# Weighing the units of a bank together, and giving transposed weights the room of the raw weights, in an attention and two-MLP kernel

## The chip, the core and the metric

One core of a Trainium2 chip runs the whole program. Its engines are TensorE (PE, with the weight loads listed apart as PEld), VectorE (DVE), ScalarE (ACT), GpSimd (POOL) and SyncE (SP), which here issues every DMA. The metric is the device time of one execution in microseconds.

## The reference

Block-causal attention feeds two MLPs that run one after the other on its output.

```python
B, H, S, D = 4, 8, 576, 64
scores = where(pos_i // 64 >= pos_j // 64, q @ k.T / sqrt(D), -1e9)
attn = exp(scores - max); attn = attn / (sum(attn) + 1e-09)
x = (attn @ v) as (B * S, H * D)         # 2304 x 512, float32
h = x @ moe_w_in                         # 512 x 2048
x = maximum(0.01 * h, h) @ moe_w_out     # 2048 x 512
h = x @ moe2_w_in
out = (h * (1 / (1 + exp(-h)))) @ moe2_w_out
```

## The kernel before

The 2304 tokens are cut into six blocks of 384. The first MLP goes block by block, and each block takes 16 steps: a step has a `first_layer` (4 chunks into the bank `h`), a gate on ACT, a split of the gated values into a rounded part `ghi` and a rest `glo`, and a `second_layer` into four banks (`acc`, `u`). Block 0 multiplies in plain float32; in the blocks 1 to 5 every product is three float32r matmuls of 384 columns (hi by lo, lo by hi, hi by hi), so that a step is 24 of them. The weights come as 64-bit words in 512 KB pieces (`convert`: raw tile `wraw`, then `cy`, `cc` on ACT and DVE). The second MLP works on products of split operands (`product`), and starts when the first ends.

While the first MLP works on block b, attention makes block b+1. It is cut into 120 **units** of up to 128 rows of scores (24 in each of the blocks 1 to 5). A unit runs through this chain: `scores` on PE into a bank `s` (two banks, one or two pieces of the keys), `row_max` on DVE, `expo` on ACT, `norm` on DVE, `p_hi` on ACT or DVE and `p_lo` on DVE (float16 parts `hl`), `turn` (a DMA transpose from `hl` to `pt`, issued by SP), and `values` on PE: three float16 matmuls for each 128 keys into the one bank `x`. Up to three units share a group (the columns of one bank `x`); when its values are in, `take` moves the bank to SBUF (`x_top`, `x_sum`), and the next group may write it. Rooms are rings in SBUF: `hl` and `pt` each hold 2304 float16 columns, and a unit of 576 keys needs 1280 in both, so they hold one such unit, or two to three of fewer keys.

Nothing is ordered by the engines themselves. A planner (`Schedule`) knows a cost for each task, a hop from engine to engine, a rank, and what each task waits for; it writes out the order of each engine once, and each engine then goes through its list in that order. A task that comes late holds all that stands behind it on its engine. SP's list holds all loads, stores and transposes. After the last unit, `end_of_attention` closes attention's rooms; the second MLP's weights (`first_pair`) are loaded into `wraw` by rank, three buffers deep.

Of the kernel before, what the change touches and what calls it, by code (L numbers as in the profile page):

```python
# [19 lines left out]
P = 128  # L20
BLK = 64
# [14 lines left out]
TURN = 0  # L36
COLD = 1.2
# [5 lines left out]
YRINGS = ("ryry", "crcr", "crcr", "crcr", "llcy", "wwww")  # L43
# [14 lines left out]
class Task:  # L58
    def __init__(self, engines, deps, rank, emit):
        self.engines, self.deps, self.rank, self.emit = engines, deps, rank, emit  # L60
        self.users, self.next, self.waits, self.ready, self.end = [], [], 0, 0.0, None
        self.lag = 0


class Schedule:
# [23 lines left out]
    def run(self):  # L89
# [140 lines left out]
def attn_mlp_mlp(  # L230
# [33 lines left out]
    raw = ctx.enter_context(tc.tile_pool(name="raw", bufs=RAWS))  # L264
# [25 lines left out]
    WIDE = {"h0": NC * NB, "h1": NC * NB, "l0": NC * NB, "l1": NC * NB, "cc": CCS * DM}  # L290
    areas, turn_cc = {}, [CCS - 1]
# [5 lines left out]
    def area(name, use, dtype=F32):  # L297

        if (name, use) not in areas:
            n = WIDE.get(name) or SLOTS.get(name, (0, 1))[1] * 2 * DM  # L300
            areas[name, use] = wp.tile([P, n], dtype, tag=name, name=name)
        return areas[name, use]
# [85 lines left out]

    raws, cys, ccs = Turns(RAWS), Turns(CYS), Turns(CCS)

    def convert(src, f, sl, rk, load_rank, to=None, slow=0, lag=0):
# [8 lines left out]
        def load():  # L400
            r = raw.tile([P, DM], I64, tag="wraw", name="wraw")
# [31 lines left out]
        t_load = dma(raw_free, load_rank, DM * P * 8, load, after=raw_after, slow=slow, lag=lag)  # L433
# [251 lines left out]
    hl_ring = ring("hl", HLR, F16)  # L685
    pt_ring = ring("pt", PTR, F16)
    st_ring = ring("st", 64, F32)
    nc.gpsimd.memset(hl_ring.tile, 0.0)
# [7 lines left out]
    class Group:  # L696


        def __init__(self):
            self.x, self.evac = None, []  # L700
# [6 lines left out]
    def attention(blk):  # L707
# [165 lines left out]
        for i in range(0, len(todo), 2):  # L873
# [18 lines left out]
            for bank in banks:  # L892
# [23 lines left out]
                for j, at, a, b, us in taken:  # L916
                    take(pair[j], both, group, at, a, b, us)
            take_pair(pair[0], both)

    def unit(parts, per, rk, group, group_before):  # L920
# [8 lines left out]
        before = units[-1] if units else None  # L929
        r_p, r_hl, r_pt = p_ring.take(n), hl_ring.take(2 * nj * P), pt_ring.take(2 * nj * rows)  # L930
        r_st = st_ring.take(8)
# [5 lines left out]
        pt = pt_ring.view(r_pt, 2 * nj * rows).rearrange("p (a b) -> p a b", b=rows)  # L937
# [3 lines left out]
        def scores(e):  # L941
            u.s = []
            for k0, k1 in cut:
                s = next_s()
                u.s.append(s)
                if native:
                    hd, c0, _ = parts[0]
                    c = c0 - hd.q0
                    k_, q_ = hd.k, hd.q
                    if len(parts) > 1:  # L950
                        k_, q_ = hd.both[:, :n], hd.both[:, n:]
                    nc.tensor.matmul(s[:, :w], q_[:, c : c + P], k_[:, k0:k1], start=True, stop=True)
                    continue
                for i, (hd, c0, _) in enumerate(parts):
                    c = c0 - hd.q0
                    for j, a in enumerate((c, hd.np + c)):
                        nc.tensor.matmul(  # L957
                            s[:, :w], hd.q[:, a : a + P], hd.k[:, k0:k1],
                            start=i + j == 0, stop=i == len(parts) - 1 and j == 1,
                        )  # L960

        def row_max(e):
            if per > BLK:
# [3 lines left out]
            else:  # L967
                for i in range(n_pieces):
                    nc.vector.reduce_max(m2[:rows, i : i + 1], u.s[i][:rows, :w], axis=AX.X)
                nc.vector.tensor_reduce(nm[:rows], m2[:rows], axis=AX.X, op=ALU.max, negate=True)  # L970

        def expo(e):
            for i, (k0, k1) in enumerate(cut):
                nc.scalar.activation(  # L974
                    p[:rows, k0:k1], u.s[i][:rows, :w], AF.Exp, bias=nm[:rows], accum_out=s2[:rows, i : i + 1]
                )
# [23 lines left out]
        def turn():  # L1000
            nc.sync.dma_start_transpose(out=pt, in_=flat[:rows])

        def values(e):
# [3 lines left out]
            for i, (hd, _, c) in enumerate(parts):  # L1007
                for j in range(nj):
# [4 lines left out]
                    hi, lo = pt[:, j, q], pt[:, nj + j, q]  # L1013
# [3 lines left out]
                    nc.tensor.matmul(g.x[:, o], a, lo, start=False, stop=j == nj - 1)  # L1017

        split = [t for hd, _, _ in parts for t in hd.split]
        deps = [*split, before.t_s if before else None]  # L1020
        deps += [o.t_exp for o in (s_users[-2:-1] if n_pieces == 1 else s_users[-2:])]
        s_users.extend([u] * n_pieces)
        m = len(parts)
        time = n_pieces * mm32(w) + 100 if native else 2 * m * n_pieces * mm(w)
        u.t_s = plan.add({"PE": time}, deps, SHORT + rk, scores)
        u.t_max = plan.add({"DVE": 165 + dve_psum(n) + 110 * (n_pieces - 1) * 2}, [u.t_s, *freed(r_st)], rk, row_max)
        deps = [u.t_max, *freed(r_p)]
        u.t_exp = plan.add({"ACT": n_pieces * act(w, True, 2)}, deps, rk, expo)
# [804 lines left out]
```

## Time and profile before

| | us |
|---|---|
| three timed runs, median (lowest, highest) | 973.56 (973.06, 973.63) |
| the profiled execution, its own time | 973.34 |
| its span, first to last instruction | 971.6 |
| PE busy, PEld busy | 945.3, 868.6 |
| DVE busy, ACT busy | 805.1, 563.7 |
| mean granted TensorE clock | 0.994 of full speed |

The profiled execution is 1.7 us longer than its span, and 0.2 us shorter than the median. A matmul's end is modelled, so rows of PE overlap, and busy time hides short stops; the distance from start to start tells more. "Idle before" is the time in which an engine stood still ahead of an instruction, with what released it. Block 1's attention runs from about 40 to 131 us, that of the blocks 2 to 5 from 137 to 517 us, and the second MLP from about 600 us to the end.

### The profile page before, as it was taken

To read this page: it belongs to the slowest core of one execution; us is meant where nothing else is said; L and a number is where in the kernel's file an instruction comes from. 1 tells how busy PE (TensorE), PEld (TensorE's weight loads), DVE (VectorE), ACT (ScalarE), POOL (GpSimd) and SP (SyncE) were. 2 spreads that over 40 slices of the span, in tenths; PEclk is the share of its full clock that TensorE was granted. 3 is DMA by queue.
4 is the path that set the end of the run, shared out by engine and by line. 5 is a ranking of instruction groups with operands and counts; after the bars stand their busy time and mean duration, and the time that the engine had idled before them with its cause. 6 is when DMAs were issued, how large, how long until landed. Compare 5 with 4: busy or idle time off the path is not lost.

```text
span 971.6 us, 18459 instructions
## 1 busy us (share of the span) xinstructions
PE 945.3 (97%) x6531; PEld 868.6 (89%) x6531; DVE 805.1 (83%) x1905; ACT 563.7 (58%) x1258; POOL 36.3 (4%) x127
## 2 busy tenths in 40 slices
PE   7899999999999999999899999999999999999997
PEld 4656567999899999998799999999999999999997
DVE  6888899888888878778682698889899999888865
ACT  6897866766777666667553666655555553221322
POOL 1000000000000001000000000000000000000000
PEclk9899999999999999999999999999999999999999
DMA  7579926676655565566930532678866553443422
GB/s 258 198 183 191 236 67 132 127 132 136 157 134 128 129 157 129 114 143 157 168 86 9 185 115 84 219 250 292 278 216 210 178 166 119 139 151 100 145 65 87
DMA packets 194588, 149.85 MB, mean 154 GB/s; under 512 B 134592, under 2 KB 172480, under 8 KB 194496
## 3 DMA queue, kind: packets, MB, share of 16 engines
q1 hardware_dynamic: 194496, 148.68, 56.6%
q8 instruction: 51, 0.84, 0.4%
q14 instruction: 41, 0.34, 0.1%
HBM read 91.49 MB, written 32.51 MB: 128 GB/s over the span
## 4 chain that ended last, share of the span: by engine, by line
PE 63%; DVE 5%; DMA 2%; issue 1%; ACT 1%; SPq 0%; DVEq 0%; ACTq 0%
PE acc L1257 9%; PE acc L1648 7%; PE s L1648 5%; PE h L1237 4%; PE h L1238 4%; PE h L1239 4%; PE u L1257 3%; PE acc L1485 3%; PE acc L1486 2%; PE acc L1487 2%; PE x L1648 2%; PE u L1648 2%; PE s L957 2%; PE s L1485 2%; PE s L1486 2%; PE s L1487 2%
## 5 line engine op out<-in xcount | busy, mean ns | idle before, releaser
L974 ACT ACTIVATE p<-s,st 128x288 f32<-128x288 f32 (+5 forms) x144 | 73.3, 511 | 40.4 <-DVE st L966 26.5
L988 ACT ACTIVATE hl<-p,st 128x576 f16<-128x576 f32 (+7 forms) x115 | 67.6, 592 | 34.1 <-DVE st L984 10.3
L993 DVE SCALAR_TENSOR_TENSOR hl<-p,st,hl 128x576 f16<-128x576 f32 (+6 forms) x120 | 71.4, 597 | 13.5 <-ACT hl L988 11.6
L1285 ACT ACTIVATE g<-h 128x384 f32<-128x384 f32 x96 | 46.6, 486 | 54.2 <-PE h L1239 47.2
L1015 PE MATMUL x<-pt,v 128*128 128x128 f16 (+1 forms) x432 | 69.4, 212 | 8.8 <-DMA pt<-hl 5.5
L1016 PE MATMUL x<-pt,v 128*128 128x128 f16 (+1 forms) x432 | 67.3, 210 | 0.0
L1257 PE MATMUL acc<-ghi,w 128*128 128x384 f32 x255 | 67.3, 340 | 0.0
L1017 PE MATMUL x<-pt,v 128*128 128x128 f16 (+1 forms) x432 | 66.1, 210 | 0.0
L957 PE MATMUL s<-k,q 128*128 128x288 f32 (+5 forms) x288 | 64.5, 330 | 0.5 <-ACT p L974 0.3
L374 DVE TENSOR_TENSOR glo<-g,ghi 128x384 fp32r<-128x384 f32 x80 | 44.2, 552 | 24.4 <-ACT ghi L363 23.5
L1237 PE MATMUL h<-h,w 128*128 128x384 f32 x180 | 60.9, 338 | 0.0
L1015 PEld LDWEIGHTS <-v 128*128 128x128 bf16 x432 | 41.3, 98 | 21.1 <-issue 10.8
L1537 ACT ACTIVATE e<-e 128x384 f32<-128x384 f32 (+1 forms) x72 | 42.7, 626 | 26.1 <-DVE e L1510 20.7
L1239 PE MATMUL h<-h,w 128*128 128x384 f32 x160 | 53.6, 335 | 0.0
L1238 PE MATMUL h<-l,w 128*128 128x384 f32 x160 | 53.6, 335 | 0.0
L374 DVE TENSOR_TENSOR v<-v 128x320 f32<-128x320 f32 (+5 forms) x112 | 44.3, 423 | 10.0 <-DMA v<-vL 9.3
L409 ACT ACTIVATE cy<-wraw 128x512 f32<-128x512 f32 x64 | 42.7, 669 | 12.2 <-DMA wraw<-w 6.4
L966 DVE TENSOR_REDUCE st<-s 128x1 f32<-128x320 f32 (+5 forms) x96 | 46.5, 485 | 3.1
L1016 PEld LDWEIGHTS <-v 128*128 128x128 bf16 x432 | 41.7, 99 | 7.9 <-issue 7.4
L957 PEld LDWEIGHTS s<-k,q 128*128 128x128 f32 x288 | 43.6, 189 | 2.7 <-ACT p L974 1.7
L1257 PEld LDWEIGHTS acc<-ghi,w 128*128 128x128 f32 x255 | 45.2, 188 | 0.3
L1017 PEld LDWEIGHTS <-v 128*128 128x128 bf16 x432 | 41.4, 98 | 0.0
(368 smaller groups left out, 3016.7 us busy)
## 6 DMA issues: line engine op xcount, KB each, us to landing
wraw<-w SPq DMA_DIRECT2D x64, 512.0 KB, 5.0
a<-g SPq DMA_DIRECT2D x64, 256.0 KB, 3.2
g<-e SPq DMA_DIRECT2D x48, 192.0 KB, 2.9
g<-e SPq DMA_DIRECT2D x24, 384.0 KB, 3.4
kqr<-kq_l SPq DMA_DIRECT2D x16, 480.0 KB, 3.6
kqr<-kq_l SPq DMA_DIRECT2D x16, 416.0 KB, 3.4
v<-vL SPq DMA_DIRECT2D x32, 160.0 KB, 3.1
y<-yT SPq DMA_DIRECT2D x12, 384.0 KB, 3.9
```

Of the source, the lines that this page charges most:

```text
L374: engine[e].tensor_tensor(lo, x, hi, op=ALU.subtract)
L957: nc.tensor.matmul(s[:, :w], hd.q[:, a : a + P], hd.k[:, k0:k1], start=i + j == 0, stop=i == len(parts) - 1 and j == 1,)
L974: nc.scalar.activation(p[:rows, k0:k1], u.s[i][:rows, :w], AF.Exp, bias=nm[:rows], accum_out=s2[:rows, i : i + 1])
L993: nc.vector.scalar_tensor_tensor(hl[:rows, 1, :n], p[:rows], rc[:rows], hl[:rows, 0, :n], op0=ALU.mult, op1=ALU.subtract)
L1015: nc.tensor.matmul(g.x[:, o], a, hi, start=j == 0, stop=False)
L1016: nc.tensor.matmul(g.x[:, o], hd.vb[:, j], hi, start=False, stop=False)
L1017: nc.tensor.matmul(g.x[:, o], a, lo, start=False, stop=j == nj - 1)
L1237: nc.tensor.matmul(h, w1_lo[s.f][:, sl], hi[:, c, : s.n], start=c == 0, stop=False)
L1238: nc.tensor.matmul(h, w1_hi[s.f][:, sl], lo[:, c, : s.n], start=False, stop=False)
L1239: nc.tensor.matmul(h, w1_hi[s.f][:, sl], hi[:, c, : s.n], start=False, stop=c == NC - 1)
L1257: nc.tensor.matmul(s.acc[c][:, : s.n], a, b, start=s.f == 0 and i == 0, stop=s.f == NF - 1 and i == 2)
L1648: nc.tensor.matmul(o, a[:, x], b, start=i == 0 and j == 0 and q == 0, stop=i == NP - 1 and q == 2, skip_group_check=True,)
```

## The change

- `values` of all units of a group becomes one task on PE (`weigh_all`), which waits for all the group's transposes and adds 85 ns (`TRANSIT`) to its planned cost. Of the 128-key slices the first comes first and the others in falling order.
- The raw weights' three buffers become one area `raw`, which serves one after another: raw first-layer weights (and stores of block 0), the transposed weights `pt` of the blocks 2 to 5 (6144 float16 columns), and the second MLP's raw weights. `turn` of the blocks 2 to 5 waits for the last raw users (`raw_done`), and loads into `raw` for the second MLP wait for `end_of_attention` (`raw_later`).
- `hl` and `pt` of block 1 lie in one tile; from block 2 on `hl` has all of it (4608 columns), and its first users wait for block 1's units (`first_units`).
- The planner takes scores and values as ready 700 ns later than its costs say (`SLACK`).
- Scores, maxima and exponentials become one task for each piece; first and second layers become two tasks of two chunks each (`CUTS`).
- `YRINGS`: the blocks 1 to 3 store through `cc` and `cy` only, block 0 through three raw buffers and one `cy`.

```diff
+TRANSIT = 85
+CUTS = ((0, 1), (2, 3))
+SLACK = 700
-YRINGS = ("ryry", "crcr", "crcr", "crcr", "llcy", "wwww")
+YRINGS = ("rrry", "cycy", "cycy", "cycy", "llcy", "wwww")
...
-                heapq.heappush(waiting, (t.ready + (self.HOLD if n else 0), order[id(t)], n, e, t))
+                heapq.heappush(waiting, (t.ready + t.slack + (self.HOLD if n else 0), order[id(t)], n, e, t))
...
+    def raw_room():
+        k = turn_raw[0] = (turn_raw[0] + 1) % RAWS
+        return area("raw", turn_raw[1])[:, k * 2 * DM : (k + 1) * 2 * DM]
...
-        t_load = dma(raw_free, load_rank, DM * P * 8, load, after=raw_after, slow=slow, lag=lag)
+        t_load = dma(raw_free, load_rank, DM * P * 8, load, after=[*raw_after, *raw_later], slow=slow, lag=lag)
...
-    hl_ring = ring("hl", HLR, F16)
-    pt_ring = ring("pt", PTR, F16)
+    halves_tile = pp.tile([P, HLR + PTR], F16, tag="hl", name="hl")
+    hl_first, hl_later = Ring(halves_tile[:, :HLR], HLR), Ring(halves_tile, HLR + PTR)
+    pt_first, pt_later = Ring(halves_tile[:, HLR:], PTR), Ring(None, 4 * DM * RAWS)
...
-                for j in range(nj):
+                order = [0, *reversed(range(1, nj))]
+                for j in order:
...
-        u.t_turn = dma([*padded_keys, *freed(r_pt)], SHORT + rk, 80640 * nj, turn, 1200)
-        evac = group_before.evac if group_before else [x0_free]
-        deps = [u.t_turn, *[t for hd, _, _ in parts for t in hd.v_ready], *evac]
-        u.t_pv = plan.add({"PE": 3 * nj * m * mm16(per)}, deps, SHORT + rk, values)
+        u.t_turn = dma([*padded_keys, *freed(r_pt)], SHORT + rk, 80640 * nj, turn, 1200, () if early else raw_done)
...
+    def weigh_all(group, before):
+        us = group.units
+        deps = [t for u in us for t in (u.t_turn, *[t for hd in u.heads for t in hd.v_ready])]
+        deps += before.evac if before else [x0_free]
+        def values(e):
+            for u in us:
+                u.values(e)
+        t = plan.add({"PE": sum(u.pv_time for u in us) + TRANSIT}, deps, SHORT + us[-1].rk, values)
+        t.slack = SLACK
...
-        s.t_g1 = in_turn(3 * NC * mm(n) if blk else NC * mm32(n), deps, rk, lambda e: first_layer(s))
+        for cs in CUTS:
+            time = len(cs) * (3 * mm(n) if blk else mm32(n))
+            s.t_g1 = in_turn(time, deps, rk, lambda e, cs=cs: first_layer(s, cs))
+            deps = []
...
+                def end(e):
+                    turn_raw[1] = "w2"
+                    att.close()
...
+                raw_later.append(end_of_attention)
...
+                    first_units[:] = first_units or [t for u in units for t in (u.t_turn, u.t_pv)]
+                    raw_done[:] = raw_done or [t for users in raws.users[-RAWS:] for t in users]
```

How the order moves, at three places. On PE, in block 4's attention: before, a head's three units (320, 448 and 576 keys) are three visits to the values with MLP work in between (`x<-pt,v` is a values matmul, `s<-k,q` scores, `h` first layer, `acc` and `u` second layer).

```order
L1239 MATMUL h<-h_850,xw 128x384
L1015 LDWEIGHTS v
L1015 MATMUL x<-pt,v 128x128
...
L1017 MATMUL x<-pt,v 128x64
L957 MATMUL s<-k,q 128x448 x2
L1257 MATMUL acc<-ghi,xw 128x384
...
L1257 MATMUL u<-glo,e 128x384
L1015 LDWEIGHTS v
L1015 MATMUL x<-pt,v 128x128
```

In the changed kernel one such head stands on PE as one visit of 36 values matmuls between a second layer and the scores (`x<-raw,v` is the same operation, now read from the shared area).

```order
L1322 MATMUL u<-glo,e 128x384
L1045 LDWEIGHTS v
L1045 MATMUL x<-raw,v 128x128
...
L1047 MATMUL x<-raw,v 128x128
L984 MATMUL s<-k,q 128x288 x2
L1302 MATMUL h<-h_857,t_1063 128x384
```

Over the whole order of PE the values take 102 visits before and 40 now; the matmuls in them are 1296 in both.

On SP, near the end of attention before: loads of the second MLP's raw weights (`wraw<-w`, 512 KB each) stand between transposes of block 5.

```order
L1001 DMA_TRANSPOSE pt<-hl 128x2x128
L402 DMA wraw<-w 128x512
L1001 DMA_TRANSPOSE pt<-hl 128x2x128
L402 DMA wraw<-w 128x512 x2
L812 DMA v<-vL 128x5x64
L1001 DMA_TRANSPOSE pt<-hl 128x4x128
```

In the changed kernel the same loads (`raw<-w`) come on SP behind the last transpose of all.

```order
L1030 DMA_TRANSPOSE raw<-hl 128x10x128
L1030 DMA_TRANSPOSE raw<-hl 128x2x128 x2
L1030 DMA_TRANSPOSE raw<-hl 128x4x128
L412 DMA raw<-w 128x512 x3
```

On SP at the start of block 2's attention before: its first transposes come ahead of block 0's four stores (`yT_59`).

```order
L1001 DMA_TRANSPOSE pt<-hl 128x6x128
L774 DMA kqr<-kq_l 128x960
L1001 DMA_TRANSPOSE pt<-hl 128x8x128
L1001 DMA_TRANSPOSE pt<-hl 128x10x128
L1001 DMA_TRANSPOSE pt<-hl 128x6x128
L812 DMA v<-vL 128x5x64
L1001 DMA_TRANSPOSE pt<-hl 128x8x128
L774 DMA kqr<-kq_l 128x960
L1344 DMA yT_59<-y 128x384 x4
```

In the changed kernel the four stores stand on SP ahead of the first transposes, and three of them read the area that the transposes then write.

```order
L796 DMA kqr<-kq_l 128x960 x3
L1415 DMA yT_59<-raw 128x384 x3
L1415 DMA yT_59<-y 128x384
L796 DMA kqr<-kq_l 128x960
L1030 DMA_TRANSPOSE raw<-hl 128x6x128
L1030 DMA_TRANSPOSE raw<-hl 128x8x128
L1030 DMA_TRANSPOSE raw<-hl 128x10x128
```

On PE the last unit's values come before with 784 of the first layer's matmuls and 760 of the second's behind them, and now with 724 and 700. Of the layers' matmuls, 64 in each are block 0's, of float32.

## Rows read from the trace of the kernel before

**Rows 1.** The page: span and busy time of each engine.
```profile
span 971.6 us, 18459 instructions
...
PE 945.3 (97%) x6531; PEld 868.6 (89%) x6531; DVE 805.1 (83%) x1905; ACT 563.7 (58%) x1258; POOL 36.3 (4%) x127
```

**Rows 2.** Busy time by stretch: length, PE, PEld, DVE, ACT, POOL, clock, DMA share, GB/s.
```profile
100.00:140.00 40.00, 40.00 (x167) 23.50 (x166) 35.79 (x90) 30.77 (x63) 0.20 (x1) 1.00 0.61 154
140.00:250.00 110.00, 108.62 (x792) 98.13 (x792) 94.29 (x259) 73.97 (x179) 9.42 (x37) 1.00 0.64 130
250.00:330.00 80.00, 77.48 (x654) 73.05 (x654) 68.26 (x218) 57.48 (x162) 7.02 (x23) 1.00 0.58 138
330.00:410.00 80.00, 79.99 (x627) 76.79 (x626) 64.69 (x191) 52.93 (x132) 7.34 (x29) 1.00 0.61 134
410.00:517.00 107.00, 101.56 (x822) 96.50 (x820) 81.35 (x251) 66.66 (x188) 6.61 (x23) 0.98 0.60 130
517.00:600.00 83.00, 83.00 (x490) 82.85 (x489) 58.86 (x121) 48.71 (x94) 0.00 (x0) 1.00 0.31 100
```

**Rows 3.** PE's waits, 140 to 520 us: total, times, longest.
```profile
PE x L1015 <- DMA pt<-hl: 5.5, 4, 4.0
PE x L1015 <- DVE x L846: 2.0, 3, 0.8
PE x L1015 <- ACT x L840: 0.6, 1, 0.6
```

**Rows 4.** Scores on PE: start, duration, what (timeline, two stretches).
```profile
346.69 0.65 PE L957 MATMUL s<-k,q 128*128 128x448 f32 x2
...
405.18 0.57 PE L957 MATMUL s<-k,q 128*128 128x448 f32 x2
```

**Rows 5.** PE around the longest wait (timeline).
```profile
467.38 0.34 PE L1239 MATMUL h<-h,e 128*128 128x384 f32 x1
471.69 0.23 PE L1015 MATMUL x<-pt,v 128*128 128x64 f16 x1 [3.97 <-DMA pt<-hl]
```

**Rows 6.** SP's queue ahead of that wait (timeline).
```profile
458.65 0.56 SPq L402 DMA_DIRECT2D wraw<-w  x1
...
460.58 1.00 SPq L402 DMA_DIRECT2D wraw<-w  x2
...
462.38 2.46 SPq L1001 DMA_TRANSPOSE pt<-hl  x1
```

**Rows 7.** Busy time and clock in that wait and behind it (as rows 2).
```profile
467.00:471.70 4.70, 0.73 (x6) 0.41 (x4) 0.49 (x1) 0.00 (x0) 0.45 (x1) 1.00 1.02 92
471.70:475.30 3.60, 3.60 (x22) 3.60 (x23) 2.65 (x6) 2.25 (x7) 0.67 (x2) 0.53 0.84 221
```

**Rows 8.** The transposes: issues, and time from issue to landing.
```profile
L1001 SPq DMA_TRANSPOSE pt<-hl x120: 1167/1237/2542, 45.8 to 513.4; - x120
...
DMA to landing us min/median/max: 2.3/3.4/9.3
```

**Rows 9.** Block 0's last second layer, its copies and its stores (timeline).
```profile
160.87 0.81 PE L1249 MATMUL u<-g,cc 128*128 128x384 f32 x2
...
162.88 1.97 SPq L1344 DMA_DIRECT2D yT<-y  x4
```

**Rows 10.** Groups of the page: busy, mean ns of one, idle before.
```profile
L974 ACT ACTIVATE p<-s,st 128x288 f32<-128x288 f32 (+5 forms) x144 | 73.3, 511 | 40.4 <-DVE st L966 26.5
L988 ACT ACTIVATE hl<-p,st 128x576 f16<-128x576 f32 (+7 forms) x115 | 67.6, 592 | 34.1 <-DVE st L984 10.3
L993 DVE SCALAR_TENSOR_TENSOR hl<-p,st,hl 128x576 f16<-128x576 f32 (+6 forms) x120 | 71.4, 597 | 13.5 <-ACT hl L988 11.6
...
L374 DVE TENSOR_TENSOR glo<-g,ghi 128x384 fp32r<-128x384 f32 x80 | 44.2, 552 | 24.4 <-ACT ghi L363 23.5
...
L966 DVE TENSOR_REDUCE st<-s 128x1 f32<-128x320 f32 (+5 forms) x96 | 46.5, 485 | 3.1
```

**Rows 11.** Busy time, 550 to 600 us (as rows 2).
```profile
550.00:600.00 50.00, 50.00 (x291) 50.00 (x290) 47.62 (x97) 35.73 (x68) 0.00 (x0) 1.00 0.39 129
```

More of the change, by code (lines that the diff above doesn't have):

```diff
@@ L915, in attention @@
                     taken += [(j, at, cut, q1, us) for j, (_, _, at) in enumerate(tails)]
-                for j, at, a, b, us in taken:
-                    take(pair[j], both, group, at, a, b, us)
+                done_by = weigh_all(group, before)
+                for j, at, a, b, _ in taken:
+                    take(pair[j], both, group, at, a, b, done_by)
             take_pair(pair[0], both)
@@ L929, in unit @@
         before = units[-1] if units else None
+        pt_ring = pt_of(parts[0][0].blk)
+        early = pt_ring is pt_first
+        hl_ring = hl_first if early else hl_later
         r_p, r_hl, r_pt = p_ring.take(n), hl_ring.take(2 * nj * P), pt_ring.take(2 * nj * rows)
+        assert not any(r is o.r_pt for r in r_pt.before for o in group.units)
         r_st = st_ring.take(8)
@@ L936, in unit, with scores, row_max @@
         hl = flat.rearrange("p (a b) -> p a b", a=2)
-        pt = pt_ring.view(r_pt, 2 * nj * rows).rearrange("p (a b) -> p a b", b=rows)
+        u.r_pt = r_pt
         units.append(u)
         native = hasattr(parts[0][0], "both")
[L941 to L963, printed above, removed]
+        u.s = [None] * n_pieces
+        def scores(e, piece):
+            k0, k1 = cut[piece]
+            s = u.s[piece] = next_s()
+            if native:
+                hd, c0, _ = parts[0]
+                c = c0 - hd.q0
+                k_, q_ = hd.k, hd.q
+                if len(parts) > 1:
+                    k_, q_ = hd.both[:, :n], hd.both[:, n:]
+                nc.tensor.matmul(s[:, :w], q_[:, c : c + P], k_[:, k0:k1], start=True, stop=True)
+                return
+            for i, (hd, c0, _) in enumerate(parts):
+                c = c0 - hd.q0
+                for j, a in enumerate((c, hd.np + c)):
+                    nc.tensor.matmul(
+                        s[:, :w], hd.q[:, a : a + P], hd.k[:, k0:k1],
+                        start=i + j == 0, stop=i == len(parts) - 1 and j == 1,
+                    )
+        def row_max(e, piece):
+            last = piece == n_pieces - 1
+            if per > BLK and last:
                 nc.vector.memset(u.s[-1][:BLK, w - BLK : w], MASKED)
@@ L1016, in values, with first, second, third @@
                     nc.tensor.matmul(g.x[:, o], hd.vb[:, j], hi, start=False, stop=False)
-                    nc.tensor.matmul(g.x[:, o], a, lo, start=False, stop=j == nj - 1)
+                    nc.tensor.matmul(g.x[:, o], a, lo, start=False, stop=j == order[-1])
         split = [t for hd, _, _ in parts for t in hd.split]
-        deps = [*split, before.t_s if before else None]
-        deps += [o.t_exp for o in (s_users[-2:-1] if n_pieces == 1 else s_users[-2:])]
-        s_users.extend([u] * n_pieces)
         m = len(parts)
-        time = n_pieces * mm32(w) + 100 if native else 2 * m * n_pieces * mm(w)
-        u.t_s = plan.add({"PE": time}, deps, SHORT + rk, scores)
-        u.t_max = plan.add({"DVE": 165 + dve_psum(n) + 110 * (n_pieces - 1) * 2}, [u.t_s, *freed(r_st)], rk, row_max)
-        deps = [u.t_max, *freed(r_p)]
-        u.t_exp = plan.add({"ACT": n_pieces * act(w, True, 2)}, deps, rk, expo)
+        t_max, s_last = [], before.t_s if before else None
+        for i in range(n_pieces):
+            def first(e, i=i):
+                scores(e, i)
+            def second(e, i=i):
+                row_max(e, i)
+            deps = [*split, *s_users[-2]] if len(s_users) > 1 else [*split]
+            time = mm32(w) + 50 if native else 2 * m * mm(w)
+            u.t_s = s_last = plan.add({"PE": time}, deps, SHORT + rk, first, [s_last] if s_last else ())
+            s_last.slack = SLACK
+            s_users.append([])
+            masked = 165 if per > BLK and i == n_pieces - 1 else 50
+            time = masked + dve_psum(w) + (150 if n_pieces > 1 and i else 0)
+            t_max.append(plan.add({"DVE": time}, [u.t_s, *t_max, *(() if i else freed(r_st))], rk, second))
+        u.t_max = t_max[-1]
+        deps = [u.t_max, *freed(r_p)]
+        for i in range(n_pieces):
+            def third(e, i=i):
+                expo(e, i)
+            u.t_exp = plan.add({"ACT": act(w, True, 2)}, deps, rk, third, [u.t_exp] if i else ())
+            s_users[i - n_pieces].append(u.t_exp)
+            deps = []
         u.t_norm = plan.add({"DVE": 290 + 90 * (n_pieces - 1)}, [u.t_exp], rk, norm)
         u.t_hi = plan.add(
-            {"ACT": act(n, False, 1), "DVE": dve2x(n, 1)}, [u.t_norm, *freed(r_hl)], rk, p_hi
+            {"ACT": act(n, False, 1), "DVE": dve2x(n, 1)}, [u.t_norm, *freed(r_hl)], rk, p_hi, () if early else first_units
         )
@@ L1312, in add_second @@
         deps = [*ready, *(outs[-1] if s.f == 0 and outs else ())]
-        s.t_g2 = in_turn(3 * NC * mm(n) if blk else NC * mm32(n), deps, rk, lambda e: second_layer(s))
+        for cs in CUTS:
+            time = len(cs) * (3 * mm(n) if blk else mm32(n))
+            s.t_g2 = in_turn(time, deps, rk, lambda e, cs=cs: second_layer(s, cs))
+            deps = []
         if blk == 0:
@@ L1751, in attn_mlp_mlp @@
             if f == 0 and blk == NBLK - 1:
[L1752 to L1754 removed]
+                def end(e):
+                    turn_raw[1] = "w2"
+                    att.close()
+                end_of_attention = plan.add({"SP": 1}, [*x_done[blk], units[-1].t_pv], -1e6, end)
+                raw_later.append(end_of_attention)
             if s.before:
```

90 lines of the change are left out of this document (54 added, 36 removed).

## The prediction

> **What bounds the kernel now.** I read the page first. PE is busy for 945.3 of 971.6 us [rows 1], so nothing that is added to DVE or ACT costs time unless PE has to wait for it, and nothing that is taken from them gains. Busy PE is not PE at its peak, so next I read what one matmul costs in a stretch where PE never waits: 291 matmuls of 384 columns in 50.00 us, 0.172 us from start to start [rows 11]. A row of one such matmul lasts 0.34 us [rows 5], so its modelled end hides the first 0.17 us of any stop behind it.
>
> Then the table by stretch: from 517 us on PE has no gap (83.00 of 83.00), while from 140 to 517 us, where attention runs beside the MLP, its idle time is 1.38 + 2.52 + 0.01 + 5.44 = 9.35 us [rows 2]. The list of PE's waits says where: 8.1 us in eight waits, all at the first values matmul of a visit, for the transpose (5.5 us) or for the bank `x` of the group before (2.0 and 0.6 us) [rows 3]. One wait is nearly half of that, 3.97 us at 471.69 [rows 5], and behind it the granted clock is 0.53 of full for 3.6 us [rows 7], which is the lower of the two levels.
>
> A third cost is seen only in durations. Two score matmuls of 448 columns take 0.65 us when they follow values and 0.57 us when they follow a first layer [rows 4]: leaving a visit costs 0.08 us. The values are float16, all else in these stretches is float32r.
>
> **The change part by part.**
>
> *Fewer visits.* The order has 102 visits before and 40 now, with the same 1296 matmuls. 62 x 0.08 = 5.0 us less. Some of the visits lie in block 0's plain float32 work, where I have no pair of rows; priced at nothing for eight of the visits removed (17 visits stand behind float32 work before, 9 now), the bound is 4.3. I take **-5.0**.
>
> *The long wait.* Ahead of it SP issued three loads of 512 KB, at 458.65 and 460.58, then the transpose at 462.38 [rows 6]; the values that need it start at 471.69, so that it landed about 9.3 us after its issue, the longest of 120 where the median is 3.4 [rows 8]. DMA is 102% busy in the wait [rows 7]. The change puts these loads behind the last transpose, so nothing of that size stands in front of one. The wait is 471.69 - 467.38 - 0.17 = 4.1 us, and 3.6 us at a clock of 0.53 lose 1.7 us: **-5.8**. Where the loads go next: they start with the last values visit, and their conversion comes nine MLP steps later on DVE (as before, behind the 65th of the 80 that have a `glo`), which is 9 x 24 x 0.172 = 37 us of PE's work. That covers three loads; without this cover they would cost some 5 us.
>
> *The other waits.* 8.1 - 3.97 = 4.1 us idle in seven waits, each with 0.17 us hidden under a modelled end: 5.3 us. The allowance places values where the plan has them ready 0.7 us earlier than it places them now. The longest of these waits is 0.8 us [rows 3], so with equal lateness three or four of them leave up to 0.3 us each. Bounds: nothing removed, all removed. I take -5.3 with 0.7 left, because the distances agree: counted in the order, with the durations above, PE's work between a unit's last score and its values is 5.9 us at the least before, and 8.2 us now, with most units over 10. The chain's rows (maximum 0.485, exponential 0.511, hi 0.592, lo 0.597 us [rows 10], transpose 3.4 [rows 8]) make 5.6 us without the small operations and the hops. The wider rooms help the same way: before, a transpose of 576 keys had to find `pt` empty, and waited for the visit before it. **-4.6**.
>
> *The new wait at block 2's start.* Its first transposes now stand on SP behind block 0's stores, and need the room that these read. Block 0's last matmul ends at 160.87 + 0.81 = 161.7; the stores are issued until 162.88 + 1.97 = 164.85 [rows 9], 3.2 us later. I have no landing of such a store in the rows; the nearest are the transposes', 2.3 at the least and 3.4 in the middle. Then come three transposes, 1.24 us each to issue and 3.4 to land [rows 8]: 3.2 + 2.3 to 3.4 + 2 x 1.24 + 3.4 = 11.4 to 12.5 us. In the order 60 layer matmuls and ten score matmuls stand between, 10.3 + 1.5 = 11.8 us. So the first visit waits 0 to 0.7 us, or near 6 us if a transpose takes 9.3 again. I take **+0.5**.
>
> *Attention gets denser.* The last visit comes 120 layer matmuls earlier, 120 x 0.172 = 20.6 us. DVE does 94.29 + 68.26 + 64.69 + 81.35 = 308.6 us in the 377 us from 140 to 517 [rows 2]. Five `glo` fewer at 0.552 [rows 10] leave 305.8, to be done in 377 - 20.6 - 13 = 343 us: 89% instead of 82%. From 100 to 140 DVE was at 35.79 of 40 us, 89%, and PE did not wait [rows 2]; from 550 to 600 it was at 95% [rows 11]. So it fits, with less to spare, and what runs late adds up where nothing idles. Bounds 0 and 9 us (DVE able to fill 87%: 305.8 / 0.87 = 351). I take **+1.5**, nearer the stretch with the same share.
>
> *At no cost.* The smaller tasks (`CUTS`, pieces) are the same instructions in another interleaving; a change between scores and MLP, both float32r, shows no step in the rows (0.57 us is two matmuls in a row behind a first layer, [rows 4]). The changed store rooms wait for stores that are a block, 16 MLP steps, older. From the first weights of the second MLP on, the order of DVE and PE is as before.
>
> The sum: 973.34 - 5.0 - 5.8 - 4.6 + 0.5 + 1.5 = 959.9 us for a profiled execution. That of before lies 0.2 us under its median, so I forecast **960**.
>
> By the Trainium skill (Perfetto Trace Analysis, Identifying the Most-Contended Engine) a busy matmul row says little, and the busy share of the weight loads tells PE's headroom. From 140 to 517 us they are busy for 344.5 of 377 us [rows 2], so by that rule 32.5 us are to be had there and the kernel could reach 941. The rows speak against it: a float32r matmul takes its 0.172 us whether the attention runs or not, and what can go is what stands in the sum.
>
> **The rivals.**
> - *DVE sets the pace* (the other side). Place: blocks 2 to 5, where the order has packed the same DVE work into less PE work. The point is where the stretch is no shorter in sum: 343 + 13.4 = 356 us, a share of 305.8 / 356 = 86%. From 140 to 330 us DVE held just (94.29 + 68.26) / 190 = 86% [rows 2]. For it: a list that is fixed beforehand never catches up. Against it: DVE's idle time there is mostly time in which its input was not there, which wider rooms shorten, and 89 and 95% are seen elsewhere. At 84% the stretch is 364 us and the time 960 + 19 = 979.
> - *A merged visit trades three short waits for one long.* PE goes on only when the last of three transposes lands. If each of the 32 visits in blocks 2 to 5 waited 0.4 us, the price is 12.8 us and the time 972.6: no change. Against it: the least distance grew from 5.9 to 8.2 us.
> - *Block 2's first visit waits for the room*, near 6 us, and the clock falls as behind the long wait (1.7 us): 960 + 7 = 967.
> - *The gain does not reach the end*: the second MLP's loads, later than before, hold its first products. The price is the whole gain, 973; against it the 37 us of cover.
> - *Weight loads leave more room*, as the rule has it: 941.
>
> **How the numbers follow.** The forecast with its bounds: nothing left over, no new wait and a fitting DVE give 973.3 - 5.0 - 5.8 - 5.3 = 957.2, and the score waits and waits too small for the list another 2 or 3 us, so 954.5; the new room's wait or DVE at 87% give 967.5. 80 in 100 for 954.5 to 967.5, with the third rival inside. Below that 3 (1 of them the weight loads). Between 967.5 and 971.6, DVE in part, 5. A difference of 0.2% (1.9 us) is about what a measurement of this kernel can tell: within it 5 (many short waits, gain not reaching the end), beyond it on the slow side 7 (DVE). Faster 88, same 5, slower 7.
>
> **What would show it.** Right: no wait over 1 us at a values matmul; a clock of 1.00 from 100 us on; the page's idle PE down from 26 to some 18 us; attention ending near 483 us instead of 517; DVE near 89% until then; second-MLP loads behind the last visit. Wrong: PE waits on `x` for the transposes growing through the blocks 3 to 5 with DVE never idle (DVE sets the pace); a gap of some us at the first visit of block 2; a gap at the first product of the second MLP. The prediction fails most easily if DVE's durations are a per cent or two above what the plan used, since 300 us of nearly full work leave no place to catch up.

## The result: slower, 986.6 us

| | before | after |
|---|---|---|
| median of four timed runs, us | 973.31 | 986.55 |
| ratio, 95% interval | | 1.0142 (1.0117 to 1.0166) |
| profiled execution, its span | 973.34, 971.6 | 989.36, 987.3 |

The profiled execution of after is the slowest of its four, 2.8 us over the median. The page answers to [rows 1]:

```profile
span 987.3 us, 18427 instructions
...
PE 949.6 (96%) x6531; PEld 868.6 (88%) x6531; DVE 809.7 (82%) x1915; ACT 560.3 (57%) x1248; POOL 36.0 (4%) x127
```

The span grew by 15.7 us, PE's busy time by 4.3. PE's idle time was to fall from 26 to 18 us; it rose to 37.7. The stretches of [rows 2], as they are now (same columns):

```profile
140.00:250.00 110.00, 105.58 (x755) 94.91 (x754) 95.37 (x254) 74.29 (x178) 8.64 (x33) 0.98 0.56 125
250.00:330.00 80.00, 72.33 (x577) 67.86 (x576) 67.46 (x214) 54.71 (x152) 6.14 (x22) 1.00 0.65 138
330.00:410.00 80.00, 77.98 (x650) 74.00 (x648) 65.02 (x188) 52.06 (x132) 7.58 (x29) 1.00 0.63 133
410.00:517.00 107.00, 100.55 (x842) 94.30 (x841) 87.17 (x275) 71.81 (x201) 7.43 (x25) 1.00 0.62 135
517.00:600.00 83.00, 83.00 (x481) 83.00 (x480) 45.76 (x90) 41.48 (x79) 0.00 (x0) 1.00 0.29 95
```

PE does 356.44 us of work from 140 to 517 us, before 367.65: the loss lies where attention runs. DVE is busy for 315.02 of 377 us, 84%, so it stood still for 62 us of them, and PE waited beside a DVE that had time. The first four of PE's waits from 140 to 520 us, against [rows 3]:

```profile
PE s L984 <- ACT p L1002: 16.2, 23, 2.2
PE h L1302 <- ACT g L1350: 1.2, 1, 1.2
PE x L1045 <- DVE x L868: 1.0, 1, 1.0
PE x L1045 <- ACT q L806: 0.7, 1, 0.7
...
```

The waits at the values are nearly gone, as forecast. In their place PE's scores wait 23 times for an exponential to free one of the two banks `s`; before, there was one such wait in the same stretch:

```profile
PE s L957 <- ACT p L974: 0.3, 1, 0.3
```

Modelled ends hide part of a wait, so I counted again from start to start: for each matmul the distance to the next one, less what is usual for its line and shape (the lower quartile). In us:

| extra time of PE | before | after | i1_all_prices (below) |
|---|---|---|---|
| until the first values | 16.7 | 19.7 | 15.6 |
| stops over 120 ns at values | 11.1 | 3.2 | 0.4 |
| the same at scores | 2.4 | 22.3 | 4.4 |
| the same elsewhere | 1.6 | 2.8 | 1.4 |
| 60 to 120 ns; less | 9.8; 2.5 | 8.9; 4.5 | 6.9; 2.6 |
| behind attention | 5.9 | 5.9 | 5.6 |

The 3.0 us more until the first values lie ahead of block 2's attention. From 40 to 100 us the mean granted clock was 0.94 before and is 0.91 after; as an estimate that costs 0.03 of 60 us, 1.8 us, and the rest stays open. The line of before, then that of after (columns of [rows 2]):

```profile
40.00:100.00 60.00, 59.57 (x253) 34.80 (x254) 50.28 (x162) 49.13 (x113) 3.10 (x8) 0.94 0.81 196
```

```profile
40.00:100.00 60.00, 58.99 (x227) 31.16 (x228) 46.41 (x164) 44.58 (x112) 2.37 (x7) 0.91 0.60 162
```

How a wait at the scores comes about shows in the timeline of after around 220 us (start, duration, engine, what, idle before):

```profile
215.68 0.16 DVE L998 TENSOR_REDUCE st<-st 128x1 f32<-128x2 f32 x1
...
215.87 0.50 ACT L1002 ACTIVATE p<-s,st 128x288 f32<-128x288 f32 x1 [2.04 <-DVE st L998]
...
216.48 0.49 ACT L862 ACTIVATE x<-x 64x384 f32<-64x384 f32 x1
...
217.00 0.55 DVE L868 SCALAR_TENSOR_TENSOR x<-x,x 64x384 f32<-64x384 f32 x1 [1.17 <-ACT x L862]
...
218.32 0.49 DVE L994 TENSOR_REDUCE st<-s 128x1 f32<-128x320 f32 x1
...
219.02 0.47 ACT L1350 ACTIVATE g<-h 128x384 f32<-128x384 f32 x1
219.53 0.52 ACT L372 ACTIVATE ghi<-g 128x384 fp32r<-128x384 f32 x1
219.96 0.51 ACT L1002 ACTIVATE p<-s,st 128x320 f32<-128x320 f32 x1
...
220.61 0.53 PE L984 MATMUL s<-k,q 128*128 128x288 f32 x2 [1.01 <-ACT p L1002]
```

ACT stands 2.04 us in front of an exponential whose maximum is late on DVE; the copy of `x` behind it is late by as much, and DVE stands 1.17 us in front of that copy; the next maximum stands behind it on DVE, its exponential behind a gate on ACT, and PE waits. Both engines idle, each for the other, in the order of their lists. A late load does the same: at 188.30 us PE's longest wait (2.21 us) goes back to ACT standing 2.19 us in front of a load of keys. Behind that wait, from 188.90 to 192.50 us, the granted clock is 0.53 of full, the lower of the two levels, as it was behind the long wait before ([rows 7]).

```profile
186.51 0.68 ACT L372 ACTIVATE k<-kqr 128x576 fp32r<-128x576 f32 x1 [2.19 <-DMA kqr<-kq_l]
...
187.63 0.53 ACT L1002 ACTIVATE p<-s,st 128x320 f32<-128x320 f32 x1
...
188.30 0.53 PE L984 MATMUL s<-k,q 128*128 128x288 f32 x2 [2.21 <-ACT p L1002]
```

### The profile page after: what moved, and what is told of

Its sections match the earlier page's. It is cut to its first block, busy times and chain, and to the rows that moved or that the text cites. A ratio compares the mean times of both kernels' runs of the same rounds, so it can differ in the third digit from the quotient of the medians.

```text
span 987.3 us, 18427 instructions
## 1 busy us (share of the span) xinstructions
PE 949.6 (96%) x6531; PEld 868.6 (88%) x6531; DVE 809.7 (82%) x1915; ACT 560.3 (57%) x1248; POOL 36.0 (4%) x127
## 4 chain that ended last, share of the span: by engine, by line
PE 46%; DVE 4%; ACT 1%; issue 1%; DMA 0%; DVEq 0%; ACTq 0%
PE acc L1719 7%; PE s L1719 5%; PE acc L1322 4%; PE acc L1556 2%; PE acc L1557 2%; PE acc L1558 2%; PE u L1719 2%; PE x L1719 2%; PE h L1303 2%; PE h L1302 2%; PE h L1304 2%; PE s L1556 2%; PE s L1557 2%; PE s L1558 2%; PE u L1322 1%
## 5 line engine op out<-in xcount | busy, mean ns | idle before, releaser
L1016 ACT ACTIVATE hl<-p,st 128x128 f16<-128x128 f32 (+7 forms) x117 | 68.9, 598 | 34.9 <-DVE st L1012 15.8
L984 PE MATMUL s<-k,q 128*128 128x288 f32 (+5 forms) x288 | 67.5, 329 | 16.4 <-ACT p L1002 16.2
L984 PEld LDWEIGHTS s<-k,q 128*128 128x128 f32 x288 | 46.3, 189 | 26.8 <-ACT p L1002 24.8
L1045 PE MATMUL x<-raw,v 128*128 128x128 f16 (+1 forms) x384 | 55.4, 211 | 2.3 <-DVE x L868 1.0
L1046 PE MATMUL x<-raw,v 128*128 128x128 f16 (+1 forms) x384 | 54.6, 210 | 0.0
L1047 PE MATMUL x<-raw,v 128*128 128x128 f16 (+1 forms) x384 | 54.1, 210 | 0.0
L419 ACT ACTIVATE cy<-raw 128x512 f32<-128x512 f32 x64 | 43.0, 671 | 16.0 <-DMA raw<-w 8.7
```

The lines of the kernel that those rows point to most:

```text
L984: nc.tensor.matmul(s[:, :w], hd.q[:, a : a + P], hd.k[:, k0:k1], start=i + j == 0, stop=i == len(parts) - 1 and j == 1,)
L1045: nc.tensor.matmul(g.x[:, o], a, hi, start=j == 0, stop=False)
L1046: nc.tensor.matmul(g.x[:, o], hd.vb[:, j], hi, start=False, stop=False)
L1047: nc.tensor.matmul(g.x[:, o], a, lo, start=False, stop=j == order[-1])
```

## The experiments

Every kernel but two is the changed one with one edit or several; ratios are to the kernel before, run on the same chip. Score waits measured are PE's stops at the scores, from start to start as in the table above (22.3 us in the changed kernel); the expectations of e1 to e4 count them by the list of waits (16.2 us). The theories at first: **A**, the margin of the scores (pieces and half layers let the order place a score just when its bank is planned free); **B**, density (the wider rooms let the plan pack the attention into less of PE's work, and DVE, ACT and DMA come late); **C**, bursts (a merged visit releases a head's copies of `x` all at once).

**e1_whole**, layers as one task again:

```diff
-CUTS = ((0, 1), (2, 3))
+CUTS = ((0, 1, 2, 3),)
```

> The changed kernel with the MLP's layers whole again (one task of four chunks on PE instead of two of two). Theory A, margin: scores now stand on PE right where the plan has their bank free, and whole layers of 2.1 us gave them room that halves of 1.0 us do not; PE's waits at scores (16.2 us in the changed kernel) fall to about half and the time to 976 to 981. Theory B, density: DVE and ACT cannot keep the pace of the new order, whatever it is cut into; waits stay at 13 us or more, time 984 to 988. Theory C, bursts: the copies out of the bank x after a merged visit hold up DVE and ACT; no change either, 984 to 988.

Measured 992.2 us, ratio 1.0195 (1.0171 to 1.0220): slower still, score waits 25.2 us. No theory's range holds it, and A's forecast fails. This order isn't a clean test of A, though: part of its stops stand in the plan itself, as shown below.

**e2_joined**, the scores of a unit one task, its maxima one, its exponentials one, as before:

```diff
-        for i in range(n_pieces):
-            def first(e, i=i):
+        def first(e):
+            for i in range(n_pieces):
                 scores(e, i)
```

> The changed kernel with scores, maxima and exponentials of a unit as one task each again, so that both pieces of 576 keys wait for both banks. Theory A: the first piece no longer runs ahead into a bank that is only just free, waits at scores fall below 8 us, 974 to 981. Theory B: 984 or more, since the pace is that of DVE and ACT. Theory C: 984 to 988.

978.8 us, 1.0058 (1.0039 to 1.0077); score waits 10.0 us, by the list 5.8 (in a profiled execution of 975.35 us). A's range.

**e3_noslack**:

```diff
-SLACK = 700
+SLACK = 0
```

> The changed kernel with an allowance of 0 instead of 700 ns. Theory A: less margin still, waits at scores rise by 5 to 10 us and waits at values come back, 991 to 998. Theory B: the pace is set elsewhere, within 3 us of the changed kernel, 984 to 989. Theory C: as B.

982.5 us, 1.0096 (1.0064 to 1.0128). In this order the allowance costs some 4 us. A's forecast, a longer time, fails; the range of B and C is missed by 1.5 us.

**e4_apart**, each unit's values as a visit of its own:

```diff
-        t = plan.add({"PE": sum(u.pv_time for u in us) + TRANSIT}, deps, SHORT + us[-1].rk, values)
+        for u in us:
+            deps = [u.t_turn, *[t for hd in u.heads for t in hd.v_ready], *evac]
+            u.t_pv = plan.add({"PE": u.pv_time + TRANSIT}, deps, SHORT + u.rk, u.values)
```

> The changed kernel with the values of each unit as a visit of its own again; rooms, pieces, halves and allowance stay. Theory C: no bursts, waits at scores fall by half or more, 976 to 981. Theory A: waits at scores stay near 16 us and some 60 visits come back at 0.08 us each, 989 to 993. Theory B: as A.

988.4 us, 1.0159 (1.0138 to 1.0180). C's time falls, and A's and B's range is missed by 0.6 us: the scores' waits halve, as C has it, but without merged visits the time is the same, only the waits change place (values 17.5 us, scores 10.7). The first two of PE's waits in e4_apart, from 140 to 520 us:

```profile
PE x L1045 <- DVE x L868: 7.7, 12, 1.4
PE s L984 <- ACT p L1002: 6.5, 12, 1.8
...
```

**f1_rooms**, the rooms alone: e1, e2, e3 and e4 together, and:

```diff
-TRANSIT = 85
+TRANSIT = 0
...
-                order = [0, *reversed(range(1, nj))]
+                order = list(range(nj))
```

> The rooms alone: shared raw area, wider hl and pt, changed store rooms; values of each unit as its own visit in rising order of slices, whole layers, a unit's scores as one task, no allowance. Theory B, density: the rooms let the plan pack attention into less of PE's work (the last visit stands behind 748 and 724 layer matmuls instead of 784 and 760 before, 724 and 700 in the changed kernel), and DVE and ACT come late for it; about half of the loss, 979 to 983. Theory A, margin of the scores: with joined scores and no allowance nothing is wrong with it, 970 to 975. Theory C, bursts after merged visits: 968 to 974.

981.8 us, 1.0089 (1.0067 to 1.0112), as B has it: the wider rooms alone lose 9 us.

**f2_rooms_merged**, f1_rooms with merged visits, and **f3_joined_noslack**, e2 and e3 together:

> The rooms and the merged visits, with whole layers, joined scores and no allowance. Theory B: the last visit stands as in the rooms alone (748 and 724), so 979 to 982, less some 4 us for the visits, 975 to 979. Theory A: 968 to 973, the gain that was forecast for the visits without the loss. Theory C: 4 us or more slower than the rooms alone.

> The changed kernel with joined scores and without the allowance, halves of layers and merged visits kept. If the two gains of 8 and 4 us add up: 974 to 976. Theory A expects that. Theory B: the order is as dense as in the changed kernel (724 and 706 layer matmuls ahead of the last visit), 982 to 985.

981.4 us, 1.0094 (1.0076 to 1.0111), and 982.5 us, 1.0108 (1.0088 to 1.0128). Merging moves waits from values (17.6 to 2.6 us) to scores (7.2 to 21.1), without a gain in the sum; every forecast for f2 is missed. The gains of e2 and e3 don't add, as B has it.

**f4_small**, the later `hl` ring at its old size:

```diff
-    ... hl_later = Ring(halves_tile[:, :HLR], HLR), Ring(halves_tile, HLR + PTR)
+    ... hl_later = Ring(halves_tile[:, :HLR], HLR), Ring(halves_tile, HLR)
```

> The changed kernel with hl from block 2 on no larger than before (2304 columns), so that a unit of 576 keys waits for the transpose of the one before it again; all else as in the changed kernel. Theory B: less dense (766 and 748), 976 to 980. Theory A: pieces and halves are as they were, 984 to 988. Theory C: 984 to 988.

975.3 us, 1.0019 (0.9997 to 1.0041), 0.7 us under B's range: one ring's size undoes nearly all of the loss.

So the room decides how far the plan runs ahead. Why should that be late on the chip? I set the planner's own times (which it works out when the kernel is built) beside the trace: start of `p_lo` on DVE, trace less plan, in us, for the units 24, 72 and 119 (i1 and h4 are below).

```
before          +12.5  +20.5  +30.6   (some 6 of the last 10 are the long wait and the clock behind it)
after           +15.6  +31.7  +44.4
f4_small        +11.3  +18.6  +25.1
h4_placebo      +14.2  +21.5  +29.8
i1_all_prices   +14.7  +15.1  +15.3
```

Two theories more. **D**: loads land later than planned. **E**: some operations are underpriced.

**g1_loads**, **g2_costs**:

```diff
-... load_v)
+... load_v, lag=1200)
-... load_kq)
+... load_kq, lag=600)
```

```diff
-t_top = plan.add(copy_on(t1 - t0, True), ...
+t_top = plan.add({"ACT": act(t1 - t0, True) + 110, "DVE": dve_psum(t1 - t0) + 110}, ...
-t_sum = plan.add({"DVE": dve_psum(t1 - t0)}, ...
+t_sum = plan.add({"DVE": dve_psum(t1 - t0) + 95}, ...
-t_klo = plan.add(on_vector(nk), ...
+t_klo = plan.add({"DVE": dve(nk) + Both(115)}, ...
```

> The changed kernel, with one thing altered in the planner: it reckons that a load of values (v) lands 1.2 us later than its old cost said, and one of keys and queries (kqr) 0.6 us later, which is nearer the trace (v: median 3.5 us from issue to landing, 5.5 at most). The attention stands as early in PE's order as in the changed kernel (718 and 700 layer matmuls ahead of the last values, there 724 and 700). Density (theory B: the time follows from how tightly the order packs the attention): 984 to 989 us, score waits 20 us or more. Late loads (theory D: DVE and ACT stand in front of a load that lands later than planned, all behind it comes late, and PE meets it at the scores; ten of the 25 long score waits that could be followed back end at such a load): 973 to 979 us, score waits under 12 us. Underpriced copies (theory E): 983 to 988 us.

> The changed kernel, with three costs in the planner raised to what the trace shows from one start to the next when nothing is awaited: the copies of a bank x (x_top on ACT, 283 ns for 64x128 where the plan has 159, and x_sum on DVE, 297 where it has 201), and the rest of the keys (k_lo on DVE, 786 ns where it has 668). The plan then spreads the attention a little (760 and 748 layer matmuls ahead of the last values, as in e2_joined, which took 978.8 us). Underpriced copies (theory E: the bursts of copies behind a merged visit take longer than planned, and the maxima and exponentials behind them are late): 972 to 977 us, score waits under 9 us. Density (B): 977 to 981 us, score waits 10 to 15 us. Late loads (D): 983 to 988 us.

982.1 us, 1.0087 (1.0069 to 1.0105), and 971.5 us, 0.9980 (0.9964 to 0.9997). g1 misses D's range by 3 us and g2 is just under E's: late loads are the smaller part, and three prices take back the whole loss. Of PE's waits from 140 to 520 us one line is left in g2_costs:

```profile
PE s L984 <- ACT p L1002: 5.2, 12, 0.6
```

**g3_small_loads** and **g4_small_joined**, f4_small with g1's edit, and with e2's:

> f4_small (the hl ring at its old size) with the later landings of g1_loads in the planner; 766 and 748 layer matmuls ahead of the last values, as in f4_small. Late loads (D): 967 to 972 us, faster than before, score waits under 7 us (f4_small 12). Density (B) and underpriced copies (E): 973 to 977 us, as f4_small.

> f4_small with the scores, maxima and exponentials of a unit as one task each, as in e2_joined; 760 and 748 layer matmuls ahead of the last values (f4_small 766 and 748). Density (B): as f4_small, 973 to 978 us, since the order is no looser. Margin of scores (A, which e2_joined alone agreed with): 966 to 971 us, with score waits under 6 us. Late loads (D): 973 to 977 us.

976.1 us, 1.0026 (1.0011 to 1.0042), and 984.3 us, 1.0112 (1.0093 to 1.0132). The first is no better than f4_small, against D. The second is 9 us worse, against all theories: a new order brings several us of its own, so that small differences between these kernels prove little.

**h1_before_costs**: g2's edit in the kernel before. **h2_copies**, **h3_klo**: its first two prices alone, its third alone. **h4_placebo**: the same planned time where the price was right:

```diff
-{"ACT": act(n, False, 1), "DVE": dve2x(n, 1)}, [u.t_norm, ...
+{"ACT": act(n, False, 1) + 85, "DVE": dve2x(n, 1)}, [u.t_norm, ...
-u.t_lo = plan.add({"DVE": dve(n, 1)}, ...
+u.t_lo = plan.add({"DVE": dve(n, 1) + Both(119)}, ...
```

> The kernel before with the three prices of g2_costs in its planner (copies of x, rest of the keys); the last values then stand behind 820 and 808 layer matmuls (before: 784 and 760). Underpriced copies that only hurt where the rooms no longer hold the attention back (theory E): 970 to 975 us, no change, since the old rooms left DVE the time. The prices are a gain of their own that has nothing to do with the change: 958 to 968 us, as much faster than before as g2_costs is faster than the changed kernel.

> Of the three prices of g2_costs only the two of the copies of x (x_top on ACT, x_sum on DVE), in the changed kernel; 736 and 712 layer matmuls ahead of the last values. Underpriced copies (E): these two carry 7.6 of the 11.3 us on DVE and all 8 us on ACT, so most of the gain of 15 us: 973 to 978 us. Density (B), read between the changed kernel (724 and 700, 986.6 us) and g2_costs (760 and 748, 971.5 us): 980 to 984 us.

> Of the three prices of g2_costs only that of the rest of the keys (k_lo on DVE); 742 and 724 layer matmuls ahead of the last values. Underpriced copies (E): the smaller part of the gain, 980 to 985 us. Density (B): 977 to 981 us.

> The changed kernel with the same planned time added where the plan was right: 85 ns to p_hi on ACT and 119 ns to p_lo on DVE of each unit (8 and 11 us in all over the 96 units of the blocks 2 to 5), the copies of x and the rest of the keys at their old prices; 736 and 724 layer matmuls ahead of the last values. It matters which operation is underpriced (E): 980 to 986 us, since the copies still run later than planned in front of the maxima. Any slack on DVE and ACT does as well (theory F: the plan is too full, not wrong at one place): 970 to 977 us. Density (B): 980 to 983 us.

h1: 967.9 us, 0.9913 (0.9882 to 0.9944). h2: 979.4, 1.0045 (1.0027 to 1.0063). h3: 979.5, 1.0045 (1.0028 to 1.0063). h4: 974.3, 0.9987 (0.9968 to 1.0005). E falls in its narrow form. By the ratios the loss of 1.4% is taken back whole by g2's prices and by time added where the price was right (h4), and to some two thirds by each half of g2's prices alone (h2, h3); E's forecasts for h2 and h3 are missed, B's holds for h3, F's for h4. What the plan lacked was slack on DVE and ACT, **theory F**. Added time also makes the order looser, but looseness alone doesn't set the time: h4 (736 and 724 layer matmuls ahead of the last values) is faster by the ratios than h3 (742 and 724) and f1_rooms (748 and 724, 1.0089), whose orders are no tighter. In h1 the old rooms gain from the prices too, in the range of the second forecast: the prices are a gain of their own. With these three prices in both, the kernel with the old rooms is the faster (0.9913 against g2's 0.9980). PE's waits in h4_placebo begin with:

```profile
PE s L984 <- ACT p L1002: 8.3, 12, 1.3
...
```

**i1_all_prices** and **i2_before_all**: the edits of g1, g2 and h4 together, in the changed kernel and in the one before.

> The changed kernel with all that gave the plan more time put together: the three prices of g2_costs, the added time of h4_placebo and the later landings of g1_loads; 802 and 784 layer matmuls ahead of the last values, looser than before (784 and 760). Slack is all that was missing (theory F): the score waits fall under 5 us, the waits at the values stay under 3 us, and the time is 958 to 965 us, what the prediction counted for fewer visits and fewer waits. The change carries a loss of its own that slack doesn't mend (three units in one visit, bursts of copies): 968 to 973 us, with score waits of 8 us or more.

> The kernel before with the same prices, added time and later landings in its planner; 832 and 808 layer matmuls ahead of the last values. It shows what the change is worth when both plans have slack. Slack is all that was missing (F): 966 to 971 us, as h1_before_costs (967.9), so that the changed kernel with the same prices is the faster by 4 to 10 us. The change brings nothing of its own: both within 2 us.

i1: **959.1 us**, 0.9831 (0.9810 to 0.9852). i2: 978.9 us, 1.0036 (1.0021 to 1.0051). i1 beats both kernels, and F's forecast holds for it. Its page, its stretch from 140 to 517 us, and all of PE's waits there:

```profile
span 959.2 us, 18421 instructions
...
PE 940.0 (98%) x6531; PEld 866.0 (90%) x6531; DVE 810.2 (84%) x1911; ACT 558.5 (58%) x1252; POOL 37.1 (4%) x127
```

```profile
140.00:517.00 377.00, 375.58 (x2979) 357.63 (x2978) 321.37 (x937) 258.16 (x676) 30.41 (x108) 1.00 0.62 132
```

```profile
PE s L984 <- ACT p L1002: 1.1, 4, 0.5
```

For the kernel before F's forecast fails (966 to 971). The first three of its waits in i2:

```profile
PE x L1015 <- DMA pt<-hl: 3.7, 5, 1.2
PE s L957 <- ACT p L974: 3.6, 1, 3.6
PE x L1015 <- DVE x L846: 3.5, 3, 2.0
...
```

The planner's own times say why. The end that it works out, PE's stops that stand in the plan already (from block 2's first `p_lo` to the last values), the lateness of unit 119 as above, and the span of the trace, in us:

```
                 planned end   planned stops   lateness    span
before              940.6            0.0         30.6      971.6
after               943.3            0.0         44.4      987.3
e1_whole            965.4           21.9         27.1      991.9
f4_small            943.9            0.5         25.1      969.3
g4_small_joined     949.4            5.1         31.4      980.8
h1_before_costs     941.0            0.4         23.8      965.6
i1_all_prices       944.2            0.7         15.3      959.2
i2_before_all       953.7           12.4         23.6      977.1
```

In all twenty kernels the span is the planned end plus this lateness, to within 3 us. So the changed kernel's loss is lateness: 13.8 us more of it at unit 119, and 2.7 us of plan. And orders that seemed unlucky stop PE by plan: e1 is slower than the changed kernel although it is 17 us less late, half of g4's loss is planned, and i2 is as late as h1 but its plan stops PE for 12.0 us more.

What the change itself is worth therefore isn't shown by one number. With all prices in both it is the faster by 2% (0.9831 against 1.0036), of which some 12 us are planned stops of the old rooms; with g2's three prices it is the slower by 0.7%; the best of each differ by 0.8% (0.9831 against h1's 0.9913), in its favour.

## Why the prediction was wrong, point by point

- *Fewer visits, -5.0.* Right. The extra time of the second matmul behind a visit fell from 7.0 to 2.9 us (98 and 36 such places): -4.1.
- *The long wait, -5.8.* Right for the wait. The 1.7 us at the lower clock came back behind the score wait at 188.30 us. No wait at the values is over 1.0 us, and the three loads left SP's queue at 512.63 us, behind the last transpose; the slowest transpose lands in 5.9 us (9.3 in [rows 8]). The 37 us of cover held: PE's extra time behind attention is 5.9 us in both.
- *The other waits, -4.6.* The values' waits fell by 11.1 - 3.2 = 7.9 us, 4.1 of them the long one: -3.8. The text of the prediction puts all waits at the values; three small ones that [rows 3] leave out add 0.9 us, one of them the 0.3 us at the scores.
- *The new room, +0.5.* Block 2's first visit, at 173.90 us, didn't wait: 0.
- *Attention gets denser, +1.5: here the prediction failed.* Its argument was capacity: 305.8 us of DVE's work in 343 us, "so it fits", with attention ending near 483 us. In its place came 19.9 us at the scores, 1.2 elsewhere and 2.0 in stops under 60 ns (differences of the table), and the last values came at 512.4 us: the plan has unit 119's `p_lo` at 462.7 us instead of 482.3, but the chip ran 44.4 us behind it instead of 30.6. (The 3.0 us before the first values lie outside the stretch that the term was about.) Work that fits can still be late. The order was packed to the planner's prices, with ACT's and DVE's lists waiting for each other, and nothing was left in which a late load or a copy that held its engine 0.1 us longer could be made good. The old ring of `hl` had been that reserve, since a unit had to wait for room (f4_small). That it is lateness and not capacity at the pace that after reached, i1_all_prices shows: DVE is busier there (321.37 of 377 us, 85%) than in after, attention ends as early (last values at 512.3 us), and PE waits 1.1 us. Whether DVE could hold the 89% of the prediction isn't shown: the most that any run reached over blocks 2 to 5 is 302.31 of 346 us, 87% (h4_placebo, 152 to 498 us).
- *At no cost.* The pieces and half layers weren't free in this order: with joined pieces (e2) the time is some 8 us less, with whole layers (e1) 6 more, where the plan itself stops PE. The allowance, counted as a gain, costs 4 (e3). These differences don't add (f3), and f1_rooms, which has none of the three, still loses 9 us.

Of the rivals, *DVE sets the pace* had the sign and, at 979, half of the loss, but not the mechanism: DVE was idle for 62 us, and the waits stood at the scores, through the two banks `s`, not at `x` for transposes. *A merged visit trades three short waits for one long* didn't come: the stops at the values are 3.2 us. Of the signs for being right, the clock (0.98 from 140 to 250 us), the idle PE, the end of attention and DVE's share all failed. The prediction's last sentence came nearest: durations above the plan's, in a plan without a place to catch up. With that place given back (i1), the stops at the values fall by 10.7 us and those under 120 ns by 2.8, and the time is 959.1 us. That it is near the 960 forecast for the change itself is luck: attention ends at 512 us there too, in an order looser than before (802 and 784 layer matmuls ahead of the last values).

*Weight loads leave more room* had a chance of 1 in 100. No kernel came near its 941 us, but its direction is borne out. The Trainium skill (Perfetto Trace Analysis, Identifying the Most-Contended Engine) judges TensorE's headroom by the arithmetic done against the peak and by the busy share of the weight loads, not by the busy share of the matmuls. This case's trace agrees in direction: from 140 to 517 us i1 has 357.63 us of weight loads where the kernel before had 344.5, 13.2 more, though PE's row had shown only 9.3 us idle. Not all of the 32.5 us was to be had.

What stays open: how much of each difference under some 10 us is the luck of an order, beyond the stops that its plan holds already; no run gave the same plan another order. Nor is the lateness told apart by its sources in full: with loads priced later (g1) unit 119 is 37.7 us late instead of 44.4.

## What to carry to other kernels

Where a program fixes each engine's order beforehand, a busy share under 100% doesn't say that the order holds: set the planned starts beside the trace, and look whether the lateness grows; and compare the planned ends, since an order can be slower in the plan already. A room that seems too small may be what leaves the plan its reserve; who widens it puts the reserve into the prices instead. And ask of every wait that is removed which bank the same lateness reaches next: here from `x` to `s`.

## What the runs showed of the hardware

An instruction's record isn't the time for which it holds its engine. In after, on ACT, an exponential of 128x288 lasts 0.50 us, and the read of its sum starts 0.39 us after it (215.87 and 216.26 us). On DVE, `p_lo` of 128x576 lasts 0.82 us and lets the next instruction start after 0.74 (197.12 us), but a clearing of part of `s` only after 0.81 (241.15 us). Some operations on 64 partitions hardly overlap with what follows: `x_sum` of 64x128 lasts 283 ns and the next starts after 297, `k_lo` of 64x576 lasts 755 ns and the next starts after 787 (medians of 32). A plan that grants every instruction the same overlap is some 0.1 us short on each of these.
